# Output stores of a fused attention and feed-forward kernel: 14 of 38 moved from SyncE's DMA queue to ScalarE's, with a new order of all operations

## The chip, the cores and the metric

The kernel runs on one core of a Trainium2 chip. A core has five engines, each with its own instruction stream, executed in order: TensorE (PE, matrix multiplies; PEld is its weight loads), VectorE (DVE), ScalarE (ACT), GpSimd (POOL) and SyncE (SP, which here only issues DMAs). They meet through semaphores. DMAs run on 16 DMA engines and are issued through queues: SP has one, ACT has one, POOL has a software one. Issuing a DMA takes time in the instruction stream of the engine that issues it. The metric is the device time of one execution, in microseconds (us).

## The reference, cut to what matters

For each of 8 batches and 8 heads there are 576 tokens of 64 values in `q`, `k` and `v`. A linear attention with exponential features is followed by a feed-forward layer with a squared ReLU:

```python
def phi(x):                                   # 64 -> 128 -> 256 features
    proj = einsum('bhsd,df->bhsf', x, w_phi)
    proj = proj - max(abs(proj), axis=-1)
    return concatenate([exp(proj), exp(-proj)], axis=-1)
q_p, k_p = phi(q), phi(k)
kv  = einsum('bhsf,bhsd->bhfd', k_p, v);  z = sum(k_p, axis=2)
x   = einsum('bhsf,bhfd->bhsd', q_p, kv) / (einsum('bhsf,bhf->bhs', q_p, z) + 1e-06)
x   = x.transpose(0, 2, 1, 3).reshape(4608, 512)
h   = maximum(x @ w_in, 0)                    # 512 -> 2048
out = h * h @ w_out                           # 2048 -> 512, float32
```

## The kernel before, in words

**Stages.** The 4608 rows are worked in nine chunks of 512. Chunks 0 to 7 are the first 512 tokens of batches 0 to 7; chunk 8 gathers the last 64 tokens of all eight. `attention(b)` makes the rows of batch b: keys and queries are loaded by POOL, turned (batches 0 and 1 on TensorE, later ones by transposing DMAs on SP, L331), projected into PSUM (L347), their maxima are taken on DVE (L405, L531) and exponentials on ACT (L411, L544). For batches 3 to 7 the query features are turned by another transposing DMA on SP (L548). The numerator is accumulated in PSUM by two groups of matmuls, `NA` and `NB` (L648), with a scaling on DVE between them (L660), and divided on DVE into a tile `xo` (L674). There are three `xo` buffers. A transposing DMA on SP (L708) turns `xo` into the input `xT` of the feed-forward.

**The feed-forward.** `ffn_in` (F1, L788) multiplies a chunk by `w_in`, 16 groups of four 128x512 matmuls, each into one PSUM bank; ACT or DVE takes the ReLU out of PSUM (L765 or L767), and DVE squares it (L774). `ffn_out` (F2, L882) makes four output tiles of 128 rows for each chunk, each accumulated over 16 matmuls in four parts. ACT or DVE copies the finished bank to one of four `ot` buffers (L195 or L193), and a DMA stores it, 256 KB, to `out` (L900; L897 for chunk 8, two stores of 128 KB per tile). That makes 38 stores, all issued by SP; the last tile of all has its own four small ones, two on SP and two on ACT (L869). PE works on three things interleaved: the attention of batch c+1, F1 of chunk c and F2 of chunk c-1.

**The order.** Nothing is scheduled on the chip. `Plan.add` numbers every operation (1680 of them) as the function creates it, and the list `ORDER` at the end of the file says in which sequence they are emitted. Each engine executes its own operations in that sequence. `STATES` has one bit for each operation that could go to either of two engines (`plan.either`): copies out of PSUM and ReLUs, ACT or DVE. `BASES` gives each PSUM tile its bank, `FILL` inserts small matmuls on a zero tile (L961) ahead of chosen operations of the start, and `GATES` holds POOL's loads of later batches back until a chosen operation is done.

**Numbers used below.** An operation's number is its place in the program's own sequence:

| number | operation |
|---|---|
| 292 | division into `xo` (L674), batch 1, fourth group of rows, DVE |
| 297, 531, 535, 539 | `NA` (L648) of batch 1's last group; parts 0 to 2 of chunk 0's fourth output tile (L882), PE |
| 464 | transposition of `xo` (L708), batch 2, fourth group, SP |
| 491, 509, 527, 545 | the four stores of chunk 0 |
| 665 | first F1 group (L788) of chunk 2, which needs 464 |
| 682, 700, 718, 736 | the four stores of chunk 1 |
| 1033, 1238 to 1242 | last transposition of `xo` for batch 5; first F1 groups of chunk 5, which need it |
| 1064 | first store of chunk 3 |
| 1137 | transposition of the keys of batch 6 (L331) |
| 1500 | last store of chunk 5 |

Of the kernel before, what the change touches and what calls it, by code (L numbers as in the profile page):

```python
# [11 lines left out]
ACT = mybir.ActivationFunctionType  # L12
# [96 lines left out]
def kernel(  # L109
# [10 lines left out]
    nc = tc.nc  # L120

    B, H, S, D = q.shape
# [8 lines left out]
    last_on, now = {}, [None]  # L131
# [51 lines left out]
    ot = ring("ot", NOT, [DM], F32)  # L183
    SL = (B * S // P - 1) % NOT
    otl = ot[SL]

    plan = Plan()
# [685 lines left out]
    def ffn_out(c, tt, part):  # L873
# [12 lines left out]
        if part == 3:  # L886
            sl = oslot[0] % NOT
            oslot[0] += 1
            def fn():
                copy(ot[sl], ps1(g))  # L890
            o = add("ACT", act_cost(512), fn, r=[g], w=[("ot", sl)], closes=g, what="ot")
            plan.either((o, "DVE", dve_cost(512)))
            for u in range(2 if c == NCH - 1 else 1):
                def fn(u=u):
                    if c == NCH - 1:
                        b = 2 * tt + u
                        pin(nc.sync.dma_start(out=out[b * S + 512 : b * S + 576, :], in_=ot[sl][u * 64 : u * 64 + 64, :]))  # L897
                    else:
                        o = out[c * S : c * S + 512, :].rearrange("(p j) n -> j p n", j=4)[tt]
                        pin(nc.sync.dma_start(out=o, in_=ot[sl]))  # L900
                add("SP", (0.5, 0), fn, r=[("ot", sl)] + [("ot", SL, half) for half in range(2) if sl == SL],
                    dma=(0.37 if c == NCH - 1 else 0.74, HW_IN, "st"), what="st")

# [204 lines left out]
```

## Time and profile before

| what | value |
|---|---|
| time, median of 3 runs (lowest to highest) | 345.33 us (344.21 to 345.71) |
| the profiled execution's own time, and its span | 346.37 us, 344.6 us |
| PE busy | 333.8 us, 97% of the span |
| DVE busy | 269.2 us, 78% |
| ACT busy | 221.6 us, 64% |
| stores on SP at L900: issue, shortest / median / longest | 0.332 / 0.570 / 1.267 us |
| stores from issue to landing, median | 3.0 us for 256 KB, 2.4 us for 128 KB |
| transpositions on SP: issue, median, and number | L331 keys 3.49 us x6, queries 2.84 us x6; L548 2.02 us x25; L708 1.27 us x28 and 1.19 us x7 |
| transposition of `xo` from issue to landing, shortest / median / longest | 2.3 / 4.7 / 7.6 us |

A share of busy time is a mean over the whole span. In the first 260 us all engines work at once; after that only F1 and F2 of the last chunks remain, and ACT, for example, is busy for 11.35 of the last 76.6 us. Issuing of DMAs is not counted as busy, so SP has no busy time at all in these tables, and a store issued by ACT will not show in ACT's busy time either. Stretches of the profile are told apart by windows of time, and a stall of PE by the view of waits, which names what ended it.

### The profile page before, as it was taken

To read this page: it belongs to the slowest core of one execution; us is meant where nothing else is said; L and a number is where in the kernel's file an instruction comes from. 1 tells how busy PE (TensorE), PEld (TensorE's weight loads), DVE (VectorE), ACT (ScalarE), POOL (GpSimd) and SP (SyncE) were. 2 spreads that over 40 slices of the span, in tenths; PEclk is the share of its full clock that TensorE was granted. 3 is DMA by queue.
4 is the path that set the end of the run, shared out by engine and by line. 5 is a ranking of instruction groups with operands and counts; after the bars stand their busy time and mean duration, and the time that the engine had idled before them with its cause. 6 is when DMAs were issued, how large, how long until landed. Compare 5 with 4: busy or idle time off the path is not lost.

```text
span 344.6 us, 8417 instructions
## 1 busy us (share of the span) xinstructions
PE 333.8 (97%) x3371; PEld 189.0 (55%) x3402; DVE 269.2 (78%) x490; ACT 221.6 (64%) x388; POOL 95.5 (28%) x143
## 2 busy tenths in 40 slices
PE   8999999799998999999999999999999999999995
PEld 7789776445554554545545554555555454444443
DVE  5999998799888798888869987798978748861540
ACT  5999996499898787577887896886376201111101
POOL 8760571952910480104604061330000000000000
PEclk9999999999999999999999999999999999999999
DMA  9999999999999999999999999999964631101115
GB/s 135 176 205 202 201 131 157 181 154 210 128 165 195 197 169 197 177 182 185 193 178 178 170 195 168 214 151 171 199 123 92 135 90 54 47 0 62 31 58 126
DMA packets 142935, 51.51 MB, mean 149 GB/s; under 512 B 111472, under 2 KB 138416, under 8 KB 142896
## 3 DMA queue, kind: packets, MB, share of 16 engines
q1 hardware_dynamic: 97488, 32.35, 51.8%
q0 software_dynamic: 44960, 18.23, 46.3%
q8 instruction: 26, 0.43, 0.6%
q10 hardware_dynamic: 448, 0.39, 0.4%
q14 instruction: 13, 0.11, 0.1%
HBM read 36.73 MB, written 9.44 MB: 134 GB/s over the span
## 4 chain that ended last, share of the span: by engine, by line
PE 86%; DVE 5%; DMA 5%; issue 2%; ACT 1%; POOL 1%; SPq 0%; DVEq 0%; POOLq 0%
PE psum L882 31%; PE psum L788 30%; PE psum L648 5%; PE psum L462 5%; PE psum L347 5%; DMA xT<-xo 3%; PE psum L827 2%; DMA kT<-xk 2%; DVE mk L405 2%; PE psum L813 1%; PE psum L799 1%; PE psum L569 1%; PE psum L846 1%; PE psum L320 1%; PE psum L450 1%
## 5 line engine op out<-in xcount | busy, mean ns | idle before, releaser
L882 PE MATMUL psum<-wout,h 128*128 128x512 bf16 x529 | 127.7, 379 | 1.7 <-issue 0.3
L788 PE MATMUL psum<-xT,win 128*128 128x512 bf16 x448 | 104.7, 379 | 1.0 <-DMA xT<-xo 1.0
L765 ACT ACTIVATE hr<-psum 128x512 bf16<-128x512 f32 x95 | 54.9, 601 | 47.9 <-DVE h L774 28.8
L882 PEld LDWEIGHTS <-h 128*128 128x128 bf16 x560 | 51.3, 98 | 56.7 <-issue 0.3
L788 PEld LDWEIGHTS <-win 128*128 128x128 bf16 x512 | 47.4, 98 | 53.6 <-DMA xT<-xo 1.4
L774 DVE TENSOR_TENSOR h<-hr 128x512 bf16<-128x512 bf16 x144 | 56.6, 415 | 10.6 <-ACT hr L765 10.2
L544 ACT ACTIVATE qf<-psum 128x1024 bf16<-128x1024 f32 (+1 forms) x50 | 45.6, 937 | 8.6 <-PE psum L347 6.1
L405 DVE TENSOR_REDUCE mk<-psum 128x8 f32<-128x1024 f32 (+1 forms) x38 | 42.3, 1119 | 4.0 <-ACT kn L411 1.9
L411 ACT ACTIVATE kn<-psum 128x1024 bf16<-128x1024 f32 (+1 forms) x38 | 36.0, 947 | 12.8 <-PE psum L347 11.1
L411 ACT ACTIVATE kp<-psum 128x1024 bf16<-128x1024 f32 (+1 forms) x38 | 35.6, 948 | 8.2 <-PE psum L347 6.6
L767 DVE TENSOR_SCALAR hr<-psum 128x512 bf16<-128x512 f32 x49 | 33.1, 684 | 9.0 <-PE psum L788 8.2
L660 DVE TENSOR_TENSOR psum<-psum,en 128x520 f32<-128x520 f32 (+1 forms) x39 | 27.2, 703 | 10.4 <-PE psum L648 6.1
L648 PEld LDWEIGHTS <-qpn 128*128 128x128 bf16 x624 | 27.0, 97 | 15.0 <-issue 3.3
L269 POOL DMA_DIRECT2D xq<-in_q_dram x24 | 17.3, 727 | 56.3 <-issue 14.0
L531 DVE TENSOR_REDUCE mq<-psum 128x8 f32<-128x1024 f32 (+1 forms) x25 | 27.8, 1113 | 6.5 <-PE psum L347 3.9
L648 PE MATMUL psum<-kv,qpn 128*128 128x65 bf16 x624 | 30.2, 193 | 1.9 <-DVE xo L674 1.7
L249 POOL DMA_DIRECT2D xk<-in_k_dram x27 | 19.9, 740 | 30.6 <-ACT en L508 15.3
L584 ACT ACTIVATE qpn<-psum 128x1024 bf16<-128x1024 f32 (+1 forms) x30 | 27.0, 956 | 1.8 <-PE psum L569 1.8
L674 DVE TENSOR_TENSOR xo<-psum,rden 128x512 bf16<-128x512 f32 (+1 forms) x39 | 26.3, 684 | 2.4 <-DMA xT<-xo 1.8
L195 ACT ACTIVATE ot<-psum 128x512 f32<-128x512 f32 x18 | 10.8, 598 | 25.7 <-PE psum L882 25.7
L249 POOL DMA_DIRECT2D xv<-in_v_dram x27 | 19.8, 740 | 14.6 <-PE psum L788 11.7
L428 DVE TENSOR_TENSOR va<-xv,va 128x1280 bf16<-128x1280 bf16 (+2 forms) x34 | 23.2, 710 | 0.0
(79 smaller groups left out, 352.8 us busy)
## 6 DMA issues: line engine op xcount, KB each, us to landing
out_dram<-ot SPq DMA_DIRECT2D x32, 256.0 KB, 3.0
xk<-in_k_dram POOLq DMA_DIRECT2D x25, 128.0 KB, 5.1
xq<-in_q_dram POOLq DMA_DIRECT2D x24, 128.0 KB, 5.1
xv<-in_v_dram POOLq DMA_DIRECT2D x24, 128.0 KB, 5.1
win<-in_moe_w_in_dram POOLq DMA_DIRECT2D x4, 512.0 KB, 10.7
wout<-in_moe_w_out_dram POOLq DMA_DIRECT2D x4, 512.0 KB, 15.5
xq<-in_q_dram POOLq DMA_DIRECT2D x4, 256.0 KB, 6.1
out_dram<-ot SPq DMA_DIRECT2D x6, 128.0 KB, 2.4
```

The costliest lines, as they stand in the source:

```text
L249: pin(nc.gpsimd.dma_start(out=x[:, m0 + a * 512 : m0 + z * 512].rearrange("p (h x) -> p h x", x=4 * D), in_=src[b][2 * a : 2 * z, 0:512, : ...
L405: pin(nc.vector.tensor_reduce(out=mk_view(g), in_=ps2(pj)[:, :, : n * Fd].rearrange("p e (i f) -> p e i f", f=Fd), axis=AX.X, op=ALU.max, ...
L411: pin(nc.scalar.activation(out=dst[slot][:, :, :n, :].rearrange("p e i f -> p e (i f)"), in_=ps2(pj)[:, :, : n * Fd], func=ACT.Exp, scale= ...
L531: pin(nc.vector.tensor_reduce(out=mqb[:, c, :, :n], in_=ps2(pj)[:, :, : n * Fd].rearrange("p e (i f) -> p e i f", f=Fd), axis=AX.X, op=ALU ...
L544: pin(nc.scalar.activation(out=o, in_=i_, func=ACT.Exp, scale=sgn))
L648: pin(nc.tensor.matmul(out=o[:, u // 4, u % 4 * D1 : (u % 4 + 1) * D1], lhsT=qpn[slot][:, sg * half + u * m : sg * half + u * m + P], rhs= ...
L660: pin(nc.vector.tensor_tensor(out=o, in0=o, in1=enb[:m, c, :].rearrange("t (b h) -> t b h", b=2).to_broadcast([m, 2, 4, D1]), op=ALU.mult))
L765: pin(nc.scalar.activation(out=hr[sl], in_=ps1(g), func=ACT.Relu))
L767: pin(nc.vector.tensor_scalar(out=hr[sl], in0=ps1(g), scalar1=0.0, scalar2=None, op0=ALU.max))
L774: pin(nc.vector.tensor_tensor(out=dst, in0=i_, in1=i_, op=ALU.mult))
L788: pin(nc.tensor.matmul(out=o, lhsT=win[mc // 4][:, kc, mc % 4 * P : (mc % 4 + 1) * P], rhs=x, start=(kc == 0), stop=(kc == KC - 1)))
L882: pin(nc.tensor.matmul(out=ps1(g), lhsT=h2[c % 2][mc // 4][:, mc % 4, tt * P : (tt + 1) * P], rhs=wout[mc // 4][:, mc % 4, :], start=(mc = ...
```

## The change

A store can now be issued by ACT: its operation gets a bit in `STATES` like the copies have, and 14 of the 38 bits are set. With 38 more groups `STATES` grows from 233 to 271 bits. `ORDER`, `BASES`, `STATES` and `FILL` are replaced by new ones; `GATES` stays, and so does the sequence of transpositions on SP.

The stores on ACT are 491 and 527 (chunk 0), 682, 700 and 736 (chunk 1), 1064 (chunk 3), 1500 (chunk 5), 1518, 1536 and 1572 (chunk 6), 1644 (chunk 7) and three of chunk 8. Counted over the whole program, ACT has 104 ReLUs in place of 95, 20 copies to `ot` in place of 18 and one copy of `kv` more; DVE has as many fewer. `FILL` holds 104 small matmuls in place of 128. Of `ORDER`, some 80 lines change; these are the ones that hold the operations named above.

```diff
                 def fn(u=u):
+                    e = nc.scalar if now[0].eng == "ACT" else nc.sync
                     if c == NCH - 1:
                         b = 2 * tt + u
-                        pin(nc.sync.dma_start(out=out[b * S + 512 : b * S + 576, :], in_=ot[sl][u * 64 : u * 64 + 64, :]))
+                        pin(e.dma_start(out=out[b * S + 512 : b * S + 576, :], in_=ot[sl][u * 64 : u * 64 + 64, :]))
                     else:
                         o = out[c * S : c * S + 512, :].rearrange("(p j) n -> j p n", j=4)[tt]
-                        pin(nc.sync.dma_start(out=o, in_=ot[sl]))
-                add("SP", (0.5, 0), fn, r=[("ot", sl)] + [("ot", SL, half) for half in range(2) if sl == SL],
+                        pin(e.dma_start(out=o, in_=ot[sl]))
+                o = add("SP", (0.5, 0), fn, r=[("ot", sl)] + [("ot", SL, half) for half in range(2) if sl == SL],
                     dma=(0.37 if c == NCH - 1 else 0.74, HW_IN, "st"), what="st")
+                plan.either((o, "ACT", (0.5, 0)))
...
 ORDER = [
...
-    553, 382, 517, 291, 376, 744, 531, 292, 377, 367, 381, 293, 297, 535, 370, 298, 378, 369, 380, 521, 552, 299,
...
-    609, 571, 568, 459, 569, 708, 745, 460, 573, 616, 461, 586, 455, 619, 690, 462, 463, 587, 468, 618, 712, 509,
-    469, 464, 578, 617, 470, 580, 694, 620, 471, 472, 716, 581, 628, 579, 640, 631, 698, 736, 621, 589, 665, 630,
-    756, 588, 683, 699, 629, 596, 666, 673, 595, 717, 677, 674, 682, 632, 667, 590, 678, 641, 591, 633, 592, 684,
...
-    1158, 1032, 1272, 1033, 1241, 1039, 1290, 1147, 1213, 1118, 1151, 1214, 1245, 1064, 1153, 1193, 1249, 1218, 1152,
...
+    517, 376, 744, 292, 531, 381, 367, 345, 293, 535, 370, 377, 380, 378, 539, 369, 256, 552, 297, 387, 298, 422,
...
+    523, 496, 502, 565, 393, 480, 397, 518, 405, 497, 540, 491, 519, 396, 511, 498, 514, 524, 545, 404, 418, 398,
...
+    609, 569, 459, 708, 745, 460, 586, 428, 573, 616, 461, 712, 618, 462, 455, 463, 468, 588, 690, 619, 464, 469,
+    578, 716, 617, 581, 509, 470, 587, 620, 694, 580, 471, 472, 698, 717, 579, 628, 640, 631, 665, 756, 682, 677,
+    629, 666, 699, 683, 589, 630, 673, 678, 632, 667, 590, 674, 679, 591, 684, 595, 592, 700, 641, 669, 594, 593,
...
+    985, 1118, 1036, 1093, 984, 994, 1027, 1109, 1037, 1026, 995, 996, 1106, 1083, 1064, 1131, 1107, 1110, 1004,
...
+    1158, 1030, 1241, 1194, 1031, 1272, 1032, 1151, 1033, 1147, 1152, 1213, 1149, 1245, 1193, 1249, 1153, 1148, 1295,
+    1214, 1150, 1253, 1039, 1182, 1273, 1168, 1299, 1160, 1170, 1254, 1328, 1159, 1169, 1242, 1154, 1171, 1250, 1243,
...
+    1437, 1481, 1349, 1372, 1354, 1438, 1404, 1359, 1500, 1355, 1439, 1231, 1356, 1405, 1433, 1357, 1358, 1464, 1230,
...
 FILL = {
-    40: (0, 26), 42: (0, 11), 74: (0, 5), 76: (0, 7), 58: (0, 10), 60: (4, 16), 92: (4, 1), 51: (6, 9), 131: (4, 8),
-    156: (3, 2), 101: (3, 23), 188: (4, 3), 134: (2, 1), 142: (5, 6),
+    40: (0, 26), 42: (0, 11), 66: (2, 5), 68: (2, 7), 60: (5, 3), 90: (0, 7), 94: (1, 10), 98: (7, 4), 92: (7, 3),
+    131: (7, 11), 156: (1, 2), 101: (1, 15),
 }
```

More of the change, by code (lines that the diff above doesn't have):

```diff
@@ L967 @@
 ORDER = [
[81 rows of a table removed]
[81 rows of a table added]
 ]
 BASES = (
-    '1455230076225145762234566476424460160675235573406256700052456706030226636000051065454425544316464174'
-    '6564062130226062232023454535230323576026604331060620046465256754235403204273004462145126042636022323'
-    '5337610104431546020330126444464066623332521736013273226062432130460664260211132331532122302014064632'
-    '10022026636324354654477457624314707106106475504327016610427251132301401205674'
+    '7010614476321000524543211440626406326060503270033006536632670136443226002400454725472052262742402460'
+    '0742402420222426465767677230612367716646246765466560460610313202231144741744002203104252466242107655'
+    '1444505477142012262427726046620632510545066430655415253002021216620666200041400510424051552153236027'
+    '34602550365674651255347472734321450503245403170546311244733410350723642775165'
 )
 STATES = (
-    '0100000001011000110001110010000100000000100011110000100100001010000000101000100000000000001011010001'
-    '1010110000001000010000010001110100000000001111000000000100011000011010001011011000101110111101101011'
-    '111111100001100010101111001011011'
+    '0101000000010100100011110011100000000000000001000000101100110000100100000000110001011000011000000100'
+    '1101001001001101100000100000000010010001100010010010000000101101000000110000011000101000100011001100'
+    '00000110000111010111011001010010010111101110000000110010000001010000011'
 )
```

148 rows, old and new, of the table ORDER are left out of this document.

## The prediction, made before the result

> **What bounds the kernel now.** I read the page's first part, then the waits of PE, then the timeline round each of those waits, then windows.
>
> ```profile
> PE 333.8 (97%) x3371; PEld 189.0 (55%) x3402; DVE 269.2 (78%) x490; ACT 221.6 (64%) x388; POOL 95.5 (28%) x143
> ```
>
> PE works all the time; what a change of order can win is PE's idle time. The waits of PE (us in total, times, longest):
>
> ```profile
> PE psum L648 <- DVE xo L674: 1.7, 1, 1.7
> PE psum L788 <- DMA xT<-xo: 1.0, 1, 1.0
> PE psum L347 <- DMA kT<-xk: 0.4, 1, 0.4
> ```
>
> These three, 3.1 us, are the only large ones after the start. The timelines (start, length) round the first and the second:
>
> ```profile
> 54.54 4.74 SPq L331 DMA_TRANSPOSE qT<-xq  x1
> 59.33 6.61 SPq L708 DMA_TRANSPOSE xT<-xo  x4
> 64.02 0.69 DVE L674 TENSOR_TENSOR xo<-psum,rden 128x512 bf16<-128x512 f32 x1 [1.83 <-DMA xT<-xo]
> 64.77 0.40 PE L648 MATMUL psum<-kv,qpn 128*128 128x65 bf16 x8 [1.67 <-DVE xo L674]
> ...
> 103.33 2.04 SPq L708 DMA_TRANSPOSE xT<-xo  x1
> 103.79 0.69 DVE L674 TENSOR_TENSOR xo<-psum,rden 128x512 bf16<-128x512 f32 x1
> 105.42 0.57 SPq L900 DMA_DIRECT2D out_dram<-ot  x1
> 106.08 1.22 SPq L708 DMA_TRANSPOSE xT<-xo  x1
> 110.79 2.55 PE L788 MATMUL psum<-xT,win 128*128 128x512 bf16 x11 [0.95 <-DMA xT<-xo]
> ```
>
> First: SP is held by the queries' transposition until 59.28, four transpositions of `xo` start late, the first lands at 63.9, and only then is its `xo` buffer free for division 292. Second: division 463, which feeds transposition 464, ends at 104.48, but SP is in the transposition before it until 105.37, then issues store 509, and only at 106.08 issues 464, for which F1 group 665 waits. The windows (length; then PE, PEld, DVE, ACT and POOL busy) show how full the engines are:
>
> ```profile
> 0.00:36.00 36.00, 33.88 (x578) 29.48 (x580) 31.38 (x68) 30.38 (x56) 19.68 (x31) 1.00 1.33 180
> 76.00:90.00 14.00, 13.95 (x162) 7.80 (x162) 13.22 (x24) 12.77 (x26) 5.66 (x9) 1.00 1.02 186
> 268.00:344.60 76.60, 72.54 (x391) 34.48 (x396) 39.63 (x82) 11.35 (x23) 0.00 (x0) 0.99 0.25 67
> ```
>
> PE idles 2.12 us in the first 36; from 76 to 90 ACT has 1.23 us free; in the last 76 it is nearly empty.
>
> **The change, part by part.** The sum is made against the profiled execution, 346.37 us (span 344.6, 1.77 around it); it lies 1.04 above the median of 345.33, and the sum is carried over to that.
>
> *SP's queue.* Each store taken away frees 0.57 us of issue and about 0.08 of gap (105.42 to 106.08 is 0.66): 14 x 0.65 = 9.1 us of SP. That is worth something only where PE waits for SP. In the new order 509 stands behind 464, so 464 is issued at 105.42: -0.66 of the 1.1 us before 665. The PE work from its last `NB` to 665 is unchanged, so the remaining 0.4 stays.
>
> *The wait for keys, 1137.* SP issues it at 181.19 behind a pile of transpositions whose sequence is unchanged. The new order puts about 0.4 us more PE work ahead of its reader: -0.4, with ends 0 and -0.55, the whole gap.
>
> *The wait at 62.7.* `NA` 297 is moved behind 535 and 539, two more parts of F2 (0.86 us each, four matmuls of 0.216), which would cover the 1.67. But `BASES` changes too: before, 297 took the PSUM banks that 292 frees; now it takes those of a key projection whose maximum, 380, comes behind 292 on DVE. 292 ends at 64.71, a square (0.41) and the maximum (1.22) follow: 66.4 in place of 64.77, 1.6 later, as much as the two parts are worth (1.73). I take -0.1; ends 0 and -1.7.
>
> *The start.* 24 fewer fillers of 0.056 us (spacing inside the 26 at the beginning) are 1.34 us of PE, but fillers only stand where PE has nothing else. There DVE and ACT set the pace (31.4 and 30.4 of 36 us), and their work is changed by a few copies and two ReLUs (0.68 on DVE, 0.60 on ACT) only. I take -0.2; ends -1.34 and +1.0, half of PE's idle time there once more.
>
> *New order of PE elsewhere.* PE's sequence is nearly the same. The place that gets tighter is F1 of chunk 5. Before, about 7.6 us of PE work lie between batch 5's last `NB` and the first F1 group; now 5.9. In the trace the last of
>
> ```profile
> 201.49 8.53 SPq L708 DMA_TRANSPOSE xT<-xo  x4
> ```
>
> is issued near 208.8 and with the median landing of 4.7 is there at 213.5; PE comes to F1 at 215.1. That lead of 1.6 is used up by the 1.7: +0.3, with ends 0 and +3.0 (landing of 7.6, the longest).
>
> *ReLUs and copies.* ACT gets 9 ReLUs x 0.601, 2 copies x 0.598 and a 0.394, DVE loses as many of 0.68 and 0.43. Counted along `ORDER`, ACT has 3 ReLUs fewer up to some 262 us and 12 more after it, where it is busy 15% of the time: nothing. Were the tail full, it would be 7 us.
>
> *Stores on ACT.* Seven fall in the last 80 us: hidden, 65 us are free there; the very last store's issue is unchanged. The other seven stand among exponentials and ReLUs, and here every one waits for its copy to `ot` and then holds ACT. An ACT issue alone, at L220, took 0.39 and 0.44 us; beside SP the two at the end share 1.38 (0.55 and 0.68) while SP's take 0.47 each:
>
> ```profile
> 340.57 1.16 SPq L869 DMA_DIRECT2D out_dram<-ot  x2
> 340.57 1.38 ACTq L869 DMA_DIRECT2D out_dram<-ot  x2
> ```
>
> None of these has a transposition beside it, as most of the seven will. Ends: 0.39, and the rest of a transposition, up to 2.93. The longest store on SP, straight behind three transpositions, is 1.27; I take 0.6, nearest to the pair. 7 x 0.6 = 4.2 us of ACT, less 3 x 0.6 for the ReLUs gone: 2.4 us over 200 us, in which ACT is idle about a fifth. Behind 682 wait a ReLU whose bank F1 needs 1.7 us of PE work later, behind 700 two copies of `kv` that `NA` needs 1.7 later, behind 1064 two ReLUs before an `NA` 1.3 later. Little of 0.6 comes through: +0.5, ends 0 and +6 (below).
>
> The pair says that two issues at once slow each other by 0.1 to 0.3 us. The Trainium skill, page Perfetto Trace Analysis, section "DMA Instruction — HWDGE (DVE, Sync)", says that an issue locks the descriptor generator for itself until all descriptors are made, and that the wait for the lock is inside the reported time. Whole serialization would have made ACT's 0.42 + 0.47 = 0.89 there, and 0.55 to 0.68 was seen, so the trace agrees in part; no run shows it with transpositions. By that page the sum would be that of the first rival.
>
> **Sum.** -0.66 -0.4 -0.1 -0.2 +0.3 +0.5 = -0.56: 346.37 becomes 345.8, and 345.33 becomes 344.8. About 0.5% (1.7 us) is what a measurement of this kernel can tell from no change, so this is no change.
>
> **The rivals.** *A: ACT is held while SP issues a transposition (slower).* In the new order 491 stands beside the queries' transposition at 79.93, 682 beside 111.80, 700 beside 115.45, 1064 beside one of a pair, 1500 beside another of L548 (2.02):
>
> ```profile
> 79.93 2.75 SPq L331 DMA_TRANSPOSE qT<-xq  x1
> 111.80 2.93 SPq L331 DMA_TRANSPOSE qT<-xq  x1
> 115.45 2.05 SPq L548 DMA_TRANSPOSE qpn<-qf  x1
> 196.45 4.95 SPq L548 DMA_TRANSPOSE qpn<-qf  x2
> ```
>
> Held for all of it, less the lead that ACT's next reader on PE has (1.2, 1.6, 1.2, 0.6, 1.6), PE loses 1.55 + 1.3 + 0.85 + 1.9 + 0.4 = 6.0; held for half, 0.85. The middle, 3.4, in place of the 0.5, gives 347.7; it decides for slower from about 2.8 us lost, stores of some 2 us. For it: ACT is 91% busy from 76 to 90. Against it: SP's own stores straight behind transpositions take 0.57. Chance 0.24.
>
> *B: a new wait on a transposition (slower).* F1 of chunk 5, or a boundary like it, gets a late landing: +3.0 in place of +0.3 gives 347.5. For it: 5.9 us against 1.0 for the division and 4.7; against: SP has fewer stores ahead. Chance 0.12.
>
> *C: the start and the waits all shrink (faster).* -0.66 -0.55 -1.7 -1.34 and nothing new: 341.1; with half of the open ones 342.8. For it: PE does nothing else there; against: the maxima behind 292 and a DVE that is full in the first 36 us. Chance 0.26.
>
> **How the numbers follow.** No change has 0.38 (343.6 to 347.1) and is the likeliest: 344.8. A and B together make slower 0.36, C faster 0.26. From C's lower half and from A's upper end (-0.56 - 0.5 + 6 = 350.3) I leave out one in ten each: 341.8 to 349.5.
>
> **What would show it.** Right: the wait of L788 on `xT` near 110 falls to about 0.4; ACT's stores among transpositions take 0.4 to 0.8 us; PE's busy time stays within 1 us. Wrong: stores on ACT of 2 us and new waits of PE on ACT's ReLUs or `kv` copies (A); a wait of L788 on `xT` near 215 (B); F1 of chunk 0 starting more than 1 us earlier, or no wait near 63 (C).

## The result, and the profile after

The kernel after takes **354.06 us** (median of four executions, 353.38 to 358.2), the kernel before beside it 345.52: a ratio of **1.028, 95% interval 1.024 to 1.032**. The forecast was 344.8 with a range up to 349.5. The profiled execution took 354.74 us, its span is 353.0, 8.4 more than before. Later executions of the same kernel fall into two groups, so from here on medians and ranges over all executions of a run are given, beside the median of the kernel before on the same chip; a ratio leaves out executions over 1.5% above the fastest of their kernel.

PE's busy time and the granted clock in 40 slices, from the page of the kernel after:

```profile
PE 334.9 (95%) x3348; PEld 188.2 (53%) x3378; DVE 263.5 (75%) x478; ACT 228.0 (65%) x400; POOL 95.6 (27%) x143
...
PEclk9999999999999978999999999999999999999999
```

PE's work is the same (334.9 against 333.8 us), but there is a stretch at a lower clock near 130 us, which the kernel before doesn't have. The waits of PE (total, times, longest):

```profile
PE psum L347 <- ACT qf L544: 5.4, 1, 5.4
PE psum L320 <- DMA xk<-in_k_dram: 1.7, 2, 1.5
PE psum L788 <- DMA xT<-xo: 1.4, 1, 1.4
```

The wait of 1.67 us at 62.7 is gone, and with it the kernel is 1.9 us ahead at the end of chunk 1's F1 (its last weights are loaded at 88.05 instead of 89.94). At the end of chunk 2's F1 the last weights are loaded at 137.43 instead of 130.43: 8.9 us are lost in between, and most of it is one new wait of 5.4 us. Its surroundings in the timeline of the kernel after (ACTq and SPq are issues of DMAs):

```profile
108.56 0.34 ACTq L901 DMA_DIRECT2D out_dram<-ot  x1
113.09 2.92 SPq L331 DMA_TRANSPOSE qT<-xq  x1
113.86 0.34 ACTq L901 DMA_DIRECT2D out_dram<-ot  x1
114.00 1.22 DVE L531 TENSOR_REDUCE mq<-psum 128x8 f32<-128x1024 f32 x1
...
115.52 1.40 POOL L269 DMA_DIRECT2D xq<-in_q_dram  x2 [13.16 <-DVE mq L531]
116.11 6.35 SPq L548 DMA_TRANSPOSE qpn<-qf  x1
...
129.60 1.09 ACT L544 ACTIVATE qf<-psum 128x512 bf16<-128x512 f32 x2 [6.06 <-DMA qpn<-qf]
...
130.73 0.82 PE L347 MATMUL psum<-wphi,kT 64*128 64x128 bf16 x12 [5.43 <-ACT qf L544]
```

Read from the bottom: the key projection 757 on PE needs PSUM banks that ACT's exponential of L544 reads; that exponential needs the buffer `qf` which transposition **632** reads; 632, issued at 116.11, takes 6.35 us to issue and lands at 129.51. In the kernel before it was issued at 115.45, took 2.05 and landed at 121.95. (608, 620 and 632 are the three transpositions of `qf` ahead of 125 us, 756 is that of the queries of batch 4.) Two things lie beside it. One is the two stores on ACT, 682 at 108.56 and 700 at 113.86. The other is POOL's **burst** of loads for batch 5: its first load, 935, waits through `GATES` for DVE's maximum 641 (L531). Here the burst opens 0.59 us ahead of 632; in the kernel before it opened 1.49 us behind it:

```profile
114.17 1.22 DVE L531 TENSOR_REDUCE mq<-psum 128x8 f32<-128x1024 f32 x1
116.94 1.40 POOL L269 DMA_DIRECT2D xq<-in_q_dram  x2 [13.96 <-issue]
```

The maximum 641 ends at nearly the same time in both traces, at 115.22 and 115.39. What differs is the time from there to POOL's first issue: 0.30 us here, 1.55 before, which the profile puts down to no wait (`<-issue`).

The windows of the kernel after (length; PE, PEld, DVE, ACT, POOL busy; granted clock, DMA share, GB/s) show what the transfers do, and what follows:

```profile
110.00:114.00 4.00, 3.19 (x14) 1.37 (x15) 3.39 (x6) 2.13 (x4) 0.00 (x0) 1.00 1.05 253
118.00:122.00 4.00, 4.00 (x44) 2.04 (x42) 3.61 (x8) 3.49 (x8) 3.45 (x5) 1.00 1.04 83
127.40:134.20 6.80, 3.47 (x25) 1.89 (x26) 1.37 (x3) 2.85 (x6) 3.27 (x5) 0.50 1.44 161
```

With transpositions and stores alone 253 GB/s are moved, with 632 and the burst 83, at the same busy share of the DMA engines. (This is the lowest such stretch: from 116 to 120 there are 157 GB/s, from 120 to 124 139.) After the idle time PE runs at half clock to 134.2; from 130.73 on that is 3.5 us at half speed, 1.7 us lost. 5.4 + 1.7 and 0.5 more at L788 (1.4 against 0.95) are 7.6 of the 8.9 us; the other 1.3 are small gaps that I have not followed, and neither have I the 1.4 us that are lost behind chunk 2. The lead of 1.9 at chunk 1 already counts a later start (first F1 at 27.25 instead of 26.67): 8.9 + 1.4 - 1.9 are the 8.4.

### The profile page after: what moved, and what is told of

It is laid out like the page before. It is cut to its first block, busy times and chain, and to the rows that moved or that the text cites. A ratio compares the mean times of both kernels' runs of the same rounds, so it can differ in the third digit from the quotient of the medians.

```text
span 353.0 us, 8376 instructions
## 1 busy us (share of the span) xinstructions
PE 334.9 (95%) x3348; PEld 188.2 (53%) x3378; DVE 263.5 (75%) x478; ACT 228.0 (65%) x400; POOL 95.6 (27%) x143
## 4 chain that ended last, share of the span: by engine, by line
PE 80%; DMA 11%; ACT 3%; issue 2%; DVE 2%; POOL 1%; SPq 0%; POOLq 0%; DVEq 0%; ACTq 0%
PE psum L882 31%; PE psum L788 27%; DMA qpn<-qf 8%; PE psum L648 5%; PE psum L347 5%; PE psum L462 4%; PE psum L827 2%; DMA xk<-in_k_dram 2%; DMA out_dram<-ot 1%; PE psum L813 1%; PE psum L569 1%; PE psum L799 1%; PE psum L846 1%; ACT qf L544 1%; PE psum L450 1%
## 5 line engine op out<-in xcount | busy, mean ns | idle before, releaser
L788 PE MATMUL psum<-xT,win 128*128 128x512 bf16 x448 | 106.0, 381 | 1.8 <-DMA xT<-xo 1.4
L765 ACT ACTIVATE hr<-psum 128x512 bf16<-128x512 f32 x104 | 61.0, 602 | 68.0 <-PE psum L788 56.1
L788 PEld LDWEIGHTS <-win 128*128 128x128 bf16 x512 | 47.1, 98 | 54.4 <-issue 1.9
L544 ACT ACTIVATE qf<-psum 128x1024 bf16<-128x1024 f32 (+1 forms) x50 | 45.8, 937 | 19.4 <-DMA qpn<-qf 10.4
L767 DVE TENSOR_SCALAR hr<-psum 128x512 bf16<-128x512 f32 x40 | 27.2, 687 | 12.5 <-PE psum L788 12.0
L269 POOL DMA_DIRECT2D xq<-in_q_dram x24 | 17.4, 729 | 56.7 <-DVE mq L531 13.2
L531 DVE TENSOR_REDUCE mq<-psum 128x8 f32<-128x1024 f32 (+1 forms) x25 | 27.8, 1112 | 4.0 <-ACT ot L195 2.0
L347 PE MATMUL psum<-wphi,kT 64*128 64x128 bf16 x276 | 13.5, 221 | 5.8 <-ACT qf L544 5.4
```

Of the source, the lines that this page charges most:

```text
L347: pin(nc.tensor.matmul(out=o[:, e, i * Fd : (i + 1) * Fd], lhsT=xt[r, t, :], rhs=wphi2[r, :], start=True, stop=True))
L531: pin(nc.vector.tensor_reduce(out=mqb[:, c, :, :n], in_=ps2(pj)[:, :, : n * Fd].rearrange("p e (i f) -> p e i f", f=Fd), axis=AX.X, op=ALU ...
L544: pin(nc.scalar.activation(out=o, in_=i_, func=ACT.Exp, scale=sgn))
L765: pin(nc.scalar.activation(out=hr[sl], in_=ps1(g), func=ACT.Relu))
L767: pin(nc.vector.tensor_scalar(out=hr[sl], in0=ps1(g), scalar1=0.0, scalar2=None, op0=ALU.max))
L788: pin(nc.tensor.matmul(out=o, lhsT=win[mc // 4][:, kc, mc % 4 * P : (mc % 4 + 1) * P], rhs=x, start=(kc == 0), stop=(kc == KC - 1)))
```

## The experiments

The first theory (**burst theory**) was: not the stores, but the burst ahead of 632 makes the loss. The rival (**stores theory**): the stores on ACT's queue make it. Where an edit changes `GATES`, the gated load and those behind it on POOL stand behind the gating operation in `ORDER`, where they did not already.

**1. A later gate in the kernel after.**

```diff
-    935: 641,
+    935: 611,
```

> The kernel after, and only POOL's burst of batch 5's loads opens later: load 935 waits for DVE's scaling 611 (near 118.5 in the trace of after) in place of the maximum 641 (115.22), with 937 and 931 behind it. The burst theory (the queue of SP's transposition 632 starves because the burst stands ahead of it): 632 takes about 2 us of issue again in place of 6.35 and lands within 5 us, PE's wait of 5.4 us in L347 and the 6.8 us at half clock go: 354.1 - 5.4 - 1.6 = 347 (346 to 348). The stores theory (the stores on ScalarE or their queue cost the time): the gate of a load changes nothing, 353.5 to 354.5.

Measured: 350.3 us (349.4 to 352.3; before 345.2). Between the two. 632 did what the burst theory says: issued 3.6 us ahead of the burst, it landed in 4.7 us, and the wait in L347 was gone:

```profile
119.64 3.25 SPq L548 DMA_TRANSPOSE qpn<-qf  x1
123.23 1.40 POOL L269 DMA_DIRECT2D xq<-in_q_dram  x2 [15.87 <-DVE psum L660]
```

The time did not follow: in this trace 5 us were lost in the start, where a wait of 2.3 us for keys was followed by 13.6 us at half clock.

**2. The new order, all stores on SP.** In `STATES` the 14 store bits are 0.

> The kernel after with its order, banks and ReLU choices, but all 38 stores issued by SP. The burst theory: the gate 641 and the transposition 632 stand as they stood, if anything 632 is issued 0.6 us later for one store more ahead of it (700 and 736): 353 to 355.5, with 632 at 6 us. The stores theory: the loss goes with the stores, about 346.

Measured: 345.1 us (344.5 to 346.6, and one execution of 350.6, which is the one with the trace; before 345.2). The burst theory as put falls: without the stores on ACT the loss is gone, with the gate unchanged.

**3. The old order, the same 14 stores on ACT.**

```diff
-ORDER, BASES, FILL and the copies' bits of STATES of after
+ORDER, BASES, FILL and the copies' bits of STATES of before
```

> The kernel before with its own order, banks and ReLU choices, and only the same 14 stores issued by ScalarE. The burst theory: ScalarE's issues cost 0.34 to 0.4 us each, hidden; SP has two stores fewer ahead of 632 near 115, which is so issued earlier, still ahead of the burst: 344.5 to 346. The stores theory: the 8 us come with the stores, 350 to 354.

Measured: 345.6 us (344.7 to 348.0; before 345.2; ratio 1.003, 1.001 to 1.006). So the stores theory falls too: neither part makes the loss alone. But the stores also fall elsewhere in the old order: the last one ahead of 632 is issued 4.6 us before it and has landed by then, where in the first trace of the kernel after it is issued 2.3 us before. ACT's issues cost it little, also beside transpositions of SP:

```profile
109.14 0.34 ACTq L901 DMA_DIRECT2D out_dram<-ot  x1
109.47 4.18 SPq L331 DMA_TRANSPOSE qT<-xq  x1
```

**4. An earlier gate in the kernel before** (`935: 677`).

> The kernel before, unchanged but for the gate of load 935: it opens with the end of F1 group 677 (about 114.3, near 1 us ahead of the issue of 632 at 115.45) in place of the maximum 641 (116.9, 1.5 us behind it). The burst theory: 632 takes about 6 us of issue and lands 8 to 9 us later than before, PE waits some 4 to 6 us in L347, with a stretch at half clock: 349 to 353. The stores theory (there are none on ScalarE here) and every theory in which the loads don't matter: 345.5, as before.

Measured: 344.8 us (343.6 to 348.9; before 345.2), no loss. But the edit did not make the condition it was for: the burst was issued 0.27 us behind 632, not ahead, and 632 landed in 6.8 us.

**5. The late gate once more.** The kernel of 1 unchanged.

> The late-gate kernel once more, for a second trace: its first trace shows 632 landing within 4.7 us and no wait in L347, but 5 us lost in the start (a wait of 2.5 us for keys at 9.4 and 13.7 us at half clock), while its other executions took 349.4 to 350.6 at a clock of 0.99 to 1.0. Lead theory (632 starves when the burst is issued less than about 0.3 us behind it; 0.4 us ahead made 6.35 us of issue, 3.6 us behind made 3.25): the trace shows a landing under 7 us again, and what the other executions lose lies elsewhere; if it lies in a wait of the start, the time is 345 to 346 whenever that wait is under 2 us. Stores theory (the early start of stores on ScalarE's queue takes the transpositions' bandwidth): 349 to 351 with waits on transpositions in other places.

Measured: 348.7 us (346.2 to 352.5; before 345.9). 632 lands in 5.7 us and PE waits 0.5 in L347. The time stays 3 us high without the half clock of the start.

**6 and 7. Which stores.** In 6 the bits of 682 and 700 are 0, the other 12 stay on ACT; in 7 only 682 and 700 are on ACT.

> The kernel after with two of the 14 stores back on SP: 682 and 700, which ScalarE issued at 108.6 and 113.9, beside 620, 756 and just ahead of 632, and which SP issues behind these. Lead theory: 632 is issued 0.66 us later for store 682 and the burst opens when it did, so 632 starves as much or more: 353 to 355. Early-stores theory (the 256 KB of these two, moved at the same time as the transpositions 620, 756 and 632, take their place on the DMA engines): 345 to 346.5. If it is others of the 14: 353 to 354.

> The kernel after with the same two stores, 682 and 700, on ScalarE and the other 12 back on SP. Lead theory: as after near 116, 352 to 355, unless a store more ahead on SP moves 632. Early-stores theory: 352 to 354 too. If it is others of the 14: 345 to 346.

Measured: 347.3 us (345.7 to 351.5) and 348.5 us (344.3 to 351.6); before 345.9. Neither is as slow as the kernel after, and neither forecast fits: both pairs add something, and executions spread. Inconclusive as to which stores.

**8. A gate earlier still in the kernel before** (`935: 665`, `931: 665`).

> The kernel before, with the gates of loads 935 and 931 on F1 group 665 (ends near 111.8 in the trace of before), some 2 us earlier than in the last such kernel, so that the burst is issued near 1.7 us ahead of 632. Lead theory: 632 takes over 6 us of issue, lands 10 to 14 us after its issue, PE waits 2 to 6 us in L347: 347.5 to 353. Stores theory: 345, since all stores are on SP.

Measured: 346.7 us (345.3 to 350.2; before 345.9; ratio 1.006, 1.002 to 1.010). Now the burst is 1.92 us ahead of 632:

```profile
111.03 1.40 POOL L269 DMA_DIRECT2D xq<-in_q_dram  x2 [9.88 <-issue]
112.95 5.54 SPq L548 DMA_TRANSPOSE qpn<-qf  x1
```

The landing of 10.1 us came as forecast, and the issue of 5.54 nearly (over 6), in the old order and with no store on ACT. But the time stayed below the forecast, and PE lost only 1.1 us at L347: a landing of 10 is nearly covered; the 13.4 of the kernel after was not.

**9 to 12. Fillers, and combinations, beside the kernel after.** Fillers are matmuls into a bank that is free at that time; nobody reads their result. 9 is the kernel after again; 10 adds fillers at the start's wait and at the wait of 757; 11 is the late gate with the first of these; 12 is 11 with all stores on SP.

```diff
 FILL = {
+    49: (0, 24), 757: (2, 70),      # 10; in 11 and 12 only 49
```

> The kernel after, unchanged, for a second trace beside the next three. Collision theory (632, the 256 KB of store 700 on ScalarE's queue and the burst all move at once): 352.5 to 355, 632 lands 11 to 14 us after its issue, PE waits 3 to 6 us in L347. If the first trace showed a rare case: 346 to 349, and no such wait.

> The kernel after with filler matmuls where PE waits: 24 ahead of transposition 49 of the start (1.3 us, where it waits 1.5 to 2.5 for keys) and 70 ahead of key projection 757 (3.9 us, where it waited 5.4); the DMAs and their order stay. If the clock, which falls to half after such waits, carries part of the loss: the waits themselves stay, no stretch at half clock, 1.5 to 2 us less than the kernel after in the common case, and no execution 4 us above the others: 351.5 to 352.5. If the waits alone carry it: as the kernel after, 353 to 354.

> The late-gate kernel with the 24 fillers ahead of transposition 49. Collision theory: with neither the burst nor the half clock of the start, what is above the kernel before is what ScalarE's stores cost in other places (1 us waits for transpositions near 110, 138 and 206): 346.5 to 348.5. If the start made the late-gate kernel slow (348.5 to 350): 345 to 346.

> The same as the run before it, but all 38 stores on SP. Collision theory: neither a store beside a transposition nor the burst ahead of 632: the order's own worth, 343.5 to 345. If the stores on ScalarE cost nothing once the burst is late: the same time as the run before it.

Measured, beside 345.5 for before: 9: 351.2 us (345.0 to 355.3); 10: 350.6 (350.0 to 354.7); 11: 350.1 (346.8 to 350.4); 12: 348.4 (347.9 to 349.1). The second trace of the kernel after is of an execution of 346.8 us: the burst is 0.52 us behind 632 there, 632 lands in 8.0 us, and PE doesn't wait in L347. So the kernel after meets the collision in some executions only. 10 doesn't size the clock term: in its trace the burst is 1.48 us behind 632, so the long wait didn't arise, and the 70 fillers took 4.07 us of PE, more than the waits at L347 that were seen at a landing near 10 us; another wait, of 2.5 us at 67.6, had 3.4 us at half clock beside it. 11 and 12 miss their forecasts by 1.6 and 3.4 us: with the late gate something else is slow, whoever issues the stores.

**13 and 14. The kernel after and the new order with all stores on SP, on one chip.**

> The kernel after once more, with many executions beside those of the next three. Two-cause theory (a transposition on SP takes 4.4 us with nothing beside it, 5.8 with a 256 KB store of ScalarE's queue, 7.5 with 400 KB and more of loads, 10.4 with both, as the traces so far have it; the time of an execution depends on how many transpositions meet them): executions spread from 345 to 355, median 350 to 353. Order theory (it is the new order alone): the same, 350 to 353.

> The kernel after with all 38 stores on SP, a second time, now on the same chip as the kernel after. Two-cause theory: no store beside a transposition, so no landing over 10.5 us and fewer waits: 345 to 347, little spread, 4 us or more under the kernel after. Order theory: within 1 us of the kernel after.

Measured: 352.5 us (345.0 to 354.7) and 345.9 us (344.5 to 348.5); before 345.1. This settles the first question: 6.6 us between two kernels that differ in the 14 stores' queue alone, and these stores cost the old order 0.4. **Both parts together make the loss.** In the trace of 14 the burst is 1.18 us behind 632 and the landing 6.3 us:

```profile
113.47 2.31 SPq L548 DMA_TRANSPOSE qpn<-qf  x1
114.65 1.40 POOL L269 DMA_DIRECT2D xq<-in_q_dram  x2 [12.46 <-DVE mq L531]
```

In that of 13 the burst is 1.1 us ahead, the landing 12.5 us, and PE waits 4.9 us in L347 with 6.8 us at half clock, as in the first trace.

**15. The earlier gate in the kernel after** (`935: 665`, `931: 665`).

> The kernel after with the gates of loads 935 and 931 on F1 group 665, so that the burst is issued near 2 us ahead of transposition 632 in every execution. Two-cause theory: store 700 and the whole burst lie beside 632 each time: it lands 11 to 14 us after its issue, PE waits 3 to 6 us in L347, mostly with a stretch at half clock, and the executions at 345 to 348 are gone: median 352 to 356. If the gate doesn't matter: as the kernel after, with its spread.

Measured: 355.4 us (354.5 to 358.2; before 345.1), and no execution is under 354. The burst now opens so early that it meets 756 first:

```profile
111.00 1.40 POOL L269 DMA_DIRECT2D xq<-in_q_dram  x2 [8.09 <-PE psum L788]
114.11 0.34 ACTq L901 DMA_DIRECT2D out_dram<-ot  x1
114.17 5.91 SPq L331 DMA_TRANSPOSE qT<-xq  x1
120.18 3.49 SPq L548 DMA_TRANSPOSE qpn<-qf  x1
```

756 takes 5.91 us of issue with the store and the burst beside it, 632 is issued 4 us late and lands at 128.8; PE waits 3.5 us in L347 and 1.8 in L450. Right in its time, though 632's own landing (8.6) was not the 11 to 14 expected.

**16. Load 745 later in the kernel after** (`745: 463` in place of 459).

> The kernel after with load 745 (64 KB of queries) gated on division 463 and placed behind it, so that it is issued after transposition 608 and not 0.4 us ahead of it; gate 641 as it was. Two-cause theory: 608 takes 1.3 to 2 us of issue instead of 3.1, SP comes to 632 up to 1.7 us earlier, in front of the burst, which then makes a landing of 6 to 8 us as in the second trace of the kernel after: median 346 to 349. If what delays SP lies elsewhere: as the kernel after.

Measured: 350.4 us (347.2 to 357.3; before 345.1). 608 took 1.77 us of issue as forecast, but in the trace (the execution of 357.3 us) SP did not come to 632 earlier: 620, beside store 682, took 4.26 and 756 3.51.

```profile
115.90 1.40 POOL L269 DMA_DIRECT2D xq<-in_q_dram  x2 [10.03 <-DVE mq L531]
117.78 5.96 SPq L548 DMA_TRANSPOSE qpn<-qf  x1
```

The burst was 1.88 us ahead, 632 took 14.0 us to land, PE waited 6.7. The median is above the 346 to 349 forecast. So load 745 isn't the origin, and the place of the burst against 632 again tells the wait.

**17 and 18. The gate half way, and the late gate in the old order.**

```diff
-    935: 641,
+    935: 675,    # 17, kernel after; 18: 611, kernel before
```

> The kernel after with the gate of load 935 on DVE's square 675, which ends 1.3 to 2 us behind the maximum 641: half way to the late gate, and about as far behind transposition 632 as the burst stood in the kernel before. Burst theory (the kernel after is slow where the burst is issued ahead of 632): a lead of 0.5 to 2 us for 632, landings of 6 to 9 us, median 346 to 349, executions above 351 rare. If 632 is not what decides: 351 to 353 as the kernel after.

> The kernel before with the late gate: load 935 waits for scaling 611, some 3 us later than the maximum 641. It tells what the late gate costs by itself: if a burst that misses 632 falls on the next transpositions of qpn (near 126) and makes the keys late, 347 to 349, and the 349 to 350 of the kernel after with the late gate are explained by 2 to 3 us of that and 2 us of stores. If the late gate costs nothing in the old order: 344.5 to 346.

Measured, beside 345.5 for before: 17: **346.7 us** (344.0 to 350.0; ratio 1.001, 0.997 to 1.004); 18: 350.1 us (347.0 to 352.8; ratio 1.012, 1.009 to 1.015). In 17 nothing but one gate differs from the kernel after, the stores on ACT included, and 6 us are back:

```profile
114.79 2.17 SPq L548 DMA_TRANSPOSE qpn<-qf  x1
116.13 1.40 POOL L269 DMA_DIRECT2D xq<-in_q_dram  x2 [14.06 <-DVE h L774]
```

And the late gate costs 4.6 us by itself, more than the 347 to 349 forecast, which is enough to account for 1, 5, 11 and 12 staying slow. In the trace of 18 the burst falls on the next pair of `qf` transpositions, of which one lands 12.2 us after its issue, and the `NA` products wait, again with 3.4 us at half clock behind it (another wait in this trace, 2.4 us in L788 at 111, comes before the burst and is not the gate's):

```profile
PE psum L648 <- DMA qpn<-qf: 2.7, 1, 2.7
```

**What the twenty traces say together.** I took from each trace when the burst was issued against 632 (minus: ahead), when 632 landed after its issue, and whether the data of a store on ACT moved during 756 or 632:

| burst against 632, us | landing of 632, no such store | landing of 632, with such a store |
|---|---|---|
| -1.92 to -0.10 | 9.6, 10.1 | 12.5, 13.4, 14.0 |
| +0.27 to +1.49 | 6.3, 6.5, 6.8, 7.0 | 6.1, 6.4, 8.0, 9.6, 10.2 |
| +3.2 to +5.1 | 4.5, 4.5 | 4.7, 5.7, 6.7 |

(15, where the burst is 9.2 us ahead, is left out.) Both causes are seen, and together they pass what PE's lead covers: it waits 1.1 to 1.5 us in L347 at landings near 10 (2, 7 and 8), and 4.9 to 6.7 at 12.5 to 14. The upper row is small, though, five traces, and one of its two without a store is of the old order. The store's part goes by 756: beside such a store it lands 7.1 us after its issue (median of 12), without one 4.7 (8), and 632 follows it on the same queue. It is no delay of SP as a whole: from the issue of 608 to that of 632 both groups take 13.4 us (medians), for SP has stores fewer. The Trainium skill, page DMA: Bandwidth & Descriptors, section "Queues, rings and completion order", says that a DMA engine takes turns between the queues that have work, packet by packet; so a store on a queue of its own moves beside the transpositions and no longer in turn with them, and the 7.1 against 4.7 agree with it.

What stays open: why one execution of the kernel after has the burst ahead and the next behind. Over its 19 executions 14 took more than 351 us, five 345.0 to 348.2 (median 352.6); of 111 executions of the kernel before, 343.8 to 351.5 us, one took more than 351.

## Why the prediction was wrong

- **Stores on ACT: this step failed.** It took +0.5, from 0.6 us of ACT per store. The issues cost 0.34 to 0.40 us (the eleven full stores; nine of them at most 0.35, under the lower end taken). What was left out is the data: 256 KB that used to take their turn among the transpositions in SP's queue now move beside them. That costs 632 about 3 us (12.5 to 14.0 in place of 9.6 to 10.1), if the burst is there too.
- **New order of PE elsewhere: the other half of it.** The step looked for PE work between an operation and its reader, and found F1 of chunk 5. It did not ask when POOL's loads open. `GATES` is unchanged, and yet the burst opens earlier against SP's transpositions. Before, it came 15.0 us after the issue of 608, in the kernels of the new order with gate 641 12.0 to 14.1 us. That used up the 1.5 us by which 632 was ahead. The larger part of it is not the gate's operation: 641 ends 13.5 us after the issue of 608 in the traces of before and of 3, and 13.2 (median) in the nine of the new order. It is POOL, whose first issue follows the gating operation by 0.3 us in all fifteen traces of the new order and by 1.5 to 1.6 in all five of the old one, whether DVE or PE ran that operation. What takes POOL 1.25 us longer in the old order is not shown.
- **Rival A was wrong in its mechanism.** ACT was not held: 0.34 us at 113.86, in the middle of SP's 2.92. The Trainium skill, page Perfetto Trace Analysis, section "DMA Instruction — HWDGE (DVE, Sync)", says that an issue waits for a lock on the descriptor generator, in its reported time; no such wait shows in these rows. The harm went the other way, from ACT's stores to SP's transpositions.
- **Rival B was right in kind, wrong in place and size.** It is a new wait on a transposition, but of `qf` for the key projection 757, not of `xo` for F1 of chunk 5; there is no wait of L788 near 215. It priced 3.0; 5.4 and 1.7 of half clock were measured. Its chance was 0.12. The lead of 1.6 us that it and the term of +0.3 started from was off, too: in the trace before, transposition 1033 landed at 214.16 and F1's weights were loaded from 214.71, a lead of 0.6.
- **SP's queue** (-0.66): 464 was issued straight behind the transposition before it, as said, but the wait of 665 was 1.4 us, not 0.4, because 608 took 3.10 us in place of 1.33 and pushed both back, and because PE came to 665 0.6 us earlier. In the traces of 9 and 14, with 608 at 1.7, the wait is gone; the step was right there.
- **The wait at 62.7** (-0.1): 1.67 went. The division 292 began at 62.99 instead of 64.02, and PE came to the `NA` products at 65.36 without a wait, so what the new bank cost stayed covered; this term was mis-sized by 1.6. **The wait for keys** (-0.4) went as said.
- **The start** (-0.2): +0.6 in its place, on the side of the upper end. A transposition of keys on PE, with less filler work ahead of it, now waits 1.5 us for a load.

The three waits forecast to shrink or go are gone in the traces of 14 and 17. The span of 14's trace is 1.9 us under that of the kernel before (342.7 against 344.6), but the medians of both, 345.9 and 346.7, lie 0.7 and 1.2 above that kernel's, and what takes the gain in other executions I have not followed. No kernel here beats the one before: 4 is at 344.8 against 345.2, ratio 0.998 (0.995 to 1.002).

## What to carry to other kernels

When a DMA is moved to another queue, follow its data as well as its issue: it stops taking its turn among that queue's transfers and starts moving beside them. When an order changes, look up in the new trace when each gated load is issued, even where its gate is unchanged, and see which transfer it now meets that an engine waits for: here one gate moved by 1.6 us was worth 6 us, and one 3.5 us later cost 4.6. Take a second and a third trace of a kernel before its loss is put down to one place.

## What the runs showed of the hardware that I had not expected

- Transpositions and loads together moved less than transpositions and stores: 83 GB/s from 118 to 122 us of the kernel after, against 253, at a DMA share of 1.04 and 1.05. Over the twenty traces a transposition of `qf` on SP lands after 4.4 us with neither loads nor a store of ACT beside it (median of 190), after 6.5 with a store (25), 7.5 with 400 KB or more of loads (51), and 10.3 with both (10). What is beside it is counted from issue to landing, so a late landing gathers more. Counted over the first 4 us after the issue, the medians are 4.5 (204), 6.2 (24) and 7.5 (30), and none has both.
- Half clock came with waits as short as 1.6 us, but not with all of them. Waits of 1.6 us (7, start), 1.8 (12) and 2.7 (18) were followed by 3.4 us at a granted clock of 0.50, the 2.3 us of 1 by 13.6; waits of 1.5 us at the start of the kernel after, of 1.7 at that of 5 and of 2.4 at 111 in 18 by none. The window of 1:

```profile
11.70:25.30 13.60, 13.29 (x135) 10.73 (x137) 9.13 (x15) 8.97 (x19) 9.73 (x13) 0.50 1.44 193
```
